# Attention and a gated feed-forward block in one kernel: stores, loads, casts and PSUM banks moved in a hand-written order

## The chip, the cores and the metric

One Trainium2 chip, one of its cores. The metric is the device time in microseconds (us) of one execution of the kernel; lower is better. The core has a matrix engine (TensorE, PE in the profile), a vector engine (VectorE, DVE), an activation engine (ScalarE, ACT), a general engine (GpSimd, POOL) and a queue engine (SyncE, SP) from which this kernel issues every DMA. Each executes its own instructions strictly in the order in which the program gives them to it; semaphores hold an instruction until its data or its buffer is there.

## The reference

```python
B, H, S, D = 8, 12, 448, 64
scores = (q @ k.T) / sqrt(D) - log(S)          # per batch b and head
attn = sigmoid(scores)
x = (attn @ v)                                  # heads side by side: 3584 tokens x 768
h = x @ w_in                                    # 768 x 2048
g = h * clip(h + 3, 0, 6) / 6
out = g @ w_out                                 # 2048 x 768, float32
```

The weights arrive as 64-bit floating-point numbers, as pairs of 32-bit words.

## The kernel before, in words

**Three stages on PE.** *Attention* is 168 steps. A step (`scores`, lines 167 to 178) multiplies one 128-wide piece of keys of a head pair with all queries into one of two PSUM score banks (tag `sc`), and ACT takes its sigmoid (line 177) into a buffer `a`. Two steps later (`LAG`) `av` (lines 180 to 205) multiplies that with the values into the PSUM bank of the head pair. After the last piece ACT copies one half of the bank (line 202), DVE adds the other half (line 203), and when three head pairs of a half batch are done, the result goes to DRAM (line 205) for batches 2 to 7.

*The first product*, x @ w_in (FFN1 below), and *the second*, g @ w_out (FFN2), are done on blocks with Strassen's scheme in Winograd's form: 7 block products M1 to M7 instead of 8, each on sums or differences of blocks. Both factors of a product are split in a rounded high part (ACT, `CAST`, line 69) and a low part (DVE, line 70), and three matmuls are done for each pair: high x high, high x low, low x high.

FFN1 is 112 slots, written out by `slots()` (lines 81 to 87): for column groups q = 0 to 15 the seven products, in an order that mixes group q+1 with the end of group q: M1(q+1), M4(q), M2(q+1), M3(q), M6(q+1), M5(q+1), M7(q+1). A slot (`product`, line 319) is 18 matmuls. M1, M6, M7 and M4 accumulate in a bank A (two buffers `sc`), M2 in a bank B, M5 and M3 in a bank D. ACT copies A after M1, M6 and M7 (lines 356 to 358; names `s`, `u`), since the next product adds to the same bank; DVE adds the copies to B or D (line 362, `cB`, `cD`), ACT takes a relu (line 353), DVE the gate (line 344), POOL two differences of the gated blocks (lines 367, 369), and SP stores them (line 349).

FFN2 is 56 units: products in the order M1, M2, M6, M7, M5, M4, M3 (`PHASES`), for each four groups p and two halves h. A unit is 36 matmuls into a bank triple `po`. Its moving part `gx` is loaded (`gr`, line 428, for M5 and M4 with two more pieces, line 433, that DVE subtracts, line 443), cast and split. After the second half DVE or ACT adds the bank to running sums (line 573 or 590) and SP stores finished outputs (line 576).

**Beside them: the weights.** `decode` (lines 46 to 64) turns the 64-bit pairs into 32-bit numbers: one ACT operation (line 50, absolute value), then six on DVE (lines 52 to 63). w_in is decoded during attention in 16 pieces (`w1_unit`, line 228; four POOL sums per two pieces, lines 75 to 78; stores, lines 242 and 243), the first half of w_out during attention (`w2_unit`, line 245), its second half in units 0 to 11 of FFN2, followed by four POOL sums (`w2_sums`, lines 528 to 531) and five stores (line 536), twice. Each piece is a generator; an `events` table calls its next stage at a given step.

**Order and buffers.** The order is by hand: every engine gets its instructions in program order. Weight loads of both kinds (`wi`, `wo`, and `ws`, `w2s` for FFN1 and FFN2) use one pool of three staging buffers (line 135); split FFN1 weights, the decoded blocks and the second pieces for M5 and M4 one ring of five (line 138). The load of slot n+5's weights is issued at slot n (line 493) and its cast and low part at slot n+2, three slots ahead of use (line 494). `at_slot` and `at_unit` are tables like `events`, for FFN1 and FFN2. A buffer that is asked for again is waited for by the first instruction that writes it.

Of the kernel before, what the change touches and what calls it, by code (L numbers as in the profile page):

```python
# [18 lines left out]
P = 128  # L19
# [47 lines left out]
def split(nc, hi, lo, a):  # L67

    nc.scalar.copy(hi, a)  # L69
    nc.vector.tensor_tensor(out=lo, in0=a, in1=hi.bitcast(F32), op=ALU.subtract)  # L70

# [19 lines left out]
def tile_kernel(ctx: ExitStack, tc: tile.TileContext, qk, vP, wi, wo, outT):  # L91
# [56 lines left out]

    ops, at, pv, xr = {}, {}, {}, {}
# [30 lines left out]
    def av(n):  # L180
        pair, c = step(n)
        a = at.pop(n)
        for p in pair:
            if p not in pv:
                pv[p] = bank(f"pv{p % 2}", 1, f"pv_{p}")
# [10 lines left out]
        if c is None or (p % 2 and c == NC - 1):  # L196
# [7 lines left out]
            if k == KC - 1 and b >= 2:  # L204
                nc.sync.dma_start(out=xd[b, u], in_=xr.pop((b, u)))
# [17 lines left out]
    def x_split(p, k):  # L223
        x = xt[k].tile([P, 2, KC, S], F32R, tag="x", name=f"x_{p}_{k}")
        split(nc, x[:, 0], x[:, 1], xr[p].pop(k))
        xts[p, k] = x

    def w1_unit(j, fh, held):
# [8 lines left out]
        if fh:  # L237
            s = ring(f"wS_{j}", [P, 4, KW], F32)
            sums(nc.gpsimd, *(a[:, k] for k in range(4)), *(s[:, k] for k in range(4)))
            yield  # L240
            q, r = divmod(j, 2)
            nc.sync.dma_start(out=dw1[q][:, :4, r], in_=a)
            nc.sync.dma_start(out=dw1[q][:, 4:, r], in_=s)

    def w2_unit(k, h, ec, held):
# [7 lines left out]
        if ec == EC - 1 and k in (A11, A12):  # L253
            nc.sync.dma_start(out=dw2[k, h], in_=held.pop((k, h)))
# [46 lines left out]
    for s in range(NS + LAG):  # L301
        if s < NS:
            scores(s)
        for f, a in events.get(s, []):
# [7 lines left out]
    later = {}  # L312

    def at_slot(n, f, *a):
        later.setdefault(n, []).append((f, a))
# [3 lines left out]
    def product(i, q, n):  # L319
# [101 lines left out]

    def g_load(n):
        if n >= len(units):
            return
        i, p, h = units[n]
        first, second = {T1: (B12, B11), T4: (B21, T2)}.get(MOVING[i], (MOVING[i], None))
        t = gset[n % 3].tile([P, FC, S], F32, tag="gr", name=f"gr_{n}")
        nc.sync.dma_start(out=t, in_=gd[p, first, h])
        others = []
        if second is not None:  # L430
            for k in range(2):
                o = ring(f"gr_{n}_{k}", [P, 2, S], F32)
                nc.sync.dma_start(out=o, in_=gd[p, second, h][:, 2 * k : 2 * k + 2])
                others.append(o)
        gr[n] = t, others

    def g_split(n):
        if n >= len(units):
            return
        t, others = gr.pop(n)  # L440
        for k, o in enumerate(others):
            part = t[:, 2 * k : 2 * k + 2]
# [234 lines left out]
```

## Time and profile before

| What | us |
|---|---|
| median of 3 runs | 1166.34 |
| lowest, highest | 1165.04, 1167.83 |
| the profiled execution's own time | 1161.64 |
| its span in the profile | 1159.8 |
| PE busy | 1101.3 (95%) |
| DVE busy | 734.7 (63%) |
| ACT busy | 557.5 (48%) |
| POOL busy | 205.8 (18%) |

How to read it: busy times count compute instructions; matmuls are pipelined, so a matmul's own duration (some 0.37 us) is longer than the time from one to the next. "A <- B: 10.2, 8, 2.4" in a view of waits says that A stood still for B for 10.2 us in total, 8 times, 2.4 at the longest. A row of the timeline has start, length, engine, line, operation, tiles (out<-in) and, in square brackets, the idle time before it and what ended it. SPq and the like are the queue's own instructions, the DMA issues among them; for them the length includes the wait. The granted clock is the share of PE's full clock.

### The profile page before, as it was taken

The page shows a single profiled execution, that of the slowest core. Times are in us where ns is not written, and L with a number is a line of the kernel's source. Part 1 is how long each engine was busy: PE and PEld are TensorE (multiplying, and loading weights), DVE is VectorE, ACT ScalarE, POOL GpSimd, SP SyncE. Part 2 cuts the span into 40 slices and gives each one's busy share as a digit, 9 for nine tenths or more (in the row PEclk, how much of TensorE's full clock was granted, in tenths as well). Part 3 has the DMA queues.
Part 4 walks back from the last instruction along what each step waited for, and adds up shares of the span by engine and source line. Part 5 has one row for each costly group of instructions (what it writes and reads, how often), then busy time and mean ns, then how long its engine had stood idle before and what let it go on. Part 6 is the DMA issues. An engine that isn't in the chain of part 4 may idle for free. (4 is left out here: it accounts for less than half of the span.)

```text
span 1159.8 us, 16568 instructions
## 1 busy us (share of the span) xinstructions
PE 1101.3 (95%) x6720; PEld 864.8 (75%) x6720; DVE 734.7 (63%) x710; ACT 557.5 (48%) x612; POOL 205.8 (18%) x90
## 2 busy tenths in 40 slices
PE   8998998999999999999999998978989999989997
PEld 3433333344898899888988997968979998979997
DVE  4579654652576788777777677848643437776531
ACT  6787776886445544645554454332232313222320
POOL 1123120000143155226221113050600000000000
PEclk9999999999999999999999999998999999999999
DMA  6866978874776777587666688956775364786641
GB/s 252 307 259 229 335 275 297 313 258 163 260 227 200 268 226 238 163 304 230 200 192 213 210 259 292 348 214 236 297 290 182 127 233 171 292 312 261 252 170 60
DMA packets 81740, 278.70 MB, mean 240 GB/s; under 512 B 7936, under 2 KB 22272, under 8 KB 81664
## 3 DMA queue, kind: packets, MB, share of 16 engines
q1 hardware_dynamic: 81664, 277.64, 68.0%
q8 instruction: 53, 0.87, 0.3%
q14 instruction: 23, 0.19, 0.0%
HBM read 190.71 MB, written 86.90 MB: 239 GB/s over the span
## 5 line engine op out<-in xcount | busy, mean ns | idle before, releaser
L634 PE MATMUL po<-gx,w 128*128 128x448 f32 x2016 | 419.9, 370 | 21.2 <-DVE w L70 10.7
L634 PEld LDWEIGHTS po<-gx,w 128*128 128x128 f32 x2016 | 380.3, 189 | 60.8 <-DVE w L70 12.8
L333 PE MATMUL A<-x,w 128*128 128x448 f32 x1152 | 241.2, 367 | 0.7 <-ACT s L358 0.7
L333 PEld LDWEIGHTS A<-x,w 128*128 128x128 f32 x1152 | 216.0, 188 | 21.3 <-ACT s L358 1.1
L69 ACT CAST gx<-gr 128x1792 fp32r<-128x1792 f32 x56 | 94.8, 1694 | 258.8 <-PE po L634 98.8
L70 DVE TENSOR_TENSOR gx<-gr,gx 128x1792 fp32r<-128x1792 f32 x56 | 122.2, 2183 | 121.7 <-ACT gx L69 121.6
L177 ACT ACTIVATE a<-sc,bias_s 128x896 f32<-128x896 f32 x168 | 168.1, 1010 | 46.6 <-PE sc L175 44.2
L70 DVE TENSOR_TENSOR w<-ws,w 128x768 fp32r<-128x768 f32 x112 | 148.4, 1334 | 53.4 <-ACT w L69 53.4
L175 PE MATMUL sc<-qk 64*64 64x448 f32 x1344 | 163.7, 549 | 18.0 <-ACT a L177 12.4
L192 PE MATMUL pv<-a,v 64*64 64x448 f32 x1344 | 163.0, 542 | 2.6 <-DVE xr L203 2.3
L333 PE MATMUL D<-x,w 128*128 128x448 f32 x576 | 126.4, 374 | 10.2 <-DVE cD L362 10.2
L333 PEld LDWEIGHTS D<-x,w 128*128 128x128 f32 x576 | 110.1, 192 | 22.7 <-issue 13.0
L175 PEld LDWEIGHTS sc<-qk 64*64 64x64 f32 x1344 | 51.9, 135 | 99.4 <-issue 56.3
L192 PEld LDWEIGHTS pv<-a,v 64*64 64x64 f32 x1344 | 53.5, 134 | 79.9 <-issue 72.8
L69 ACT CAST w<-ws 128x768 fp32r<-128x768 f32 x112 | 92.1, 828 | 19.9 <-DMA ws<-dw 19.8
L367 POOL TENSOR_TENSOR gT<-g,g 128x896 f32<-128x896 f32 x16 | 43.8, 2735 | 287.2 <-DVE g L344 181.8
L353 ACT ACTIVATE g<-cD,bias 128x896 f32<-128x896 f32 x32 | 33.5, 1045 | 77.6 <-issue 39.1
L203 DVE TENSOR_TENSOR xr<-pv,y 128x448 f32<-128x448 f32 x48 | 29.8, 621 | 53.8 <-ACT y L202 53.6
L333 PE MATMUL B<-x,w 128*128 128x448 f32 x288 | 61.4, 366 | 0.0
L333 PEld LDWEIGHTS B<-x,w 128*128 128x128 f32 x288 | 54.1, 188 | 4.7
L344 DVE SCALAR_TENSOR_TENSOR g<-g,cD 128x896 f32<-128x896 f32 x32 | 46.4, 1451 | 16.2 <-ACT g L353 16.2
L358 ACT COPY u<-A 128x896 f32<-128x896 f32 x32 | 28.9, 904 | 46.9 <-PE A L333 46.9
(57 smaller groups left out, 741.6 us busy)
## 6 DMA issues: line engine op xcount, KB each, us to landing
gr<-gd SPq DMA_DIRECT2D x56, 896.0 KB, 6.0
ws<-dw SPq DMA_DIRECT2D x112, 384.0 KB, 4.0
gd<-g SPq DMA_DIRECT2D x64, 448.0 KB, 4.7
qk<-qk SPq DMA_DIRECT2D x48, 448.0 KB, 6.7
gd<-gT SPq DMA_DIRECT2D x32, 448.0 KB, 4.7
gr<-gd SPq DMA_DIRECT2D x32, 448.0 KB, 6.6
wi<-wi SPq DMA_DIRECT2D x16, 768.0 KB, 8.0
wo<-wo SPq DMA_DIRECT2D x24, 512.0 KB, 6.2
```

The source lines that it names most:

```text
L69: nc.scalar.copy(hi, a)
L70: nc.vector.tensor_tensor(out=lo, in0=a, in1=hi.bitcast(F32), op=ALU.subtract)
L175: nc.tensor.matmul(out, k[halves[r], at_k], q[halves[r]], start=True, stop=True)
L177: nc.scalar.activation(a, sc[:, :, :S], AF.Sigmoid, bias=bias_s, scale=scale)
L192: nc.tensor.matmul(pv[p][halves[j], r, :S], v, a[halves[r], int(r != j) if c is None else j], start=first, stop=last)
L203: nc.vector.tensor_tensor(out=xr[b, u][:, k], in0=pv[p][:, 1, :S], in1=y, op=ALU.add)
L333: nc.tensor.matmul(t[:, j, :S], w[:, wk, j, kc], x[:, xk, kc], start=i in (M1, M2, M5) and m == 0, stop=m == 3 * KC - 1, skip_group_check= ...
L344: nc.vector.scalar_tensor_tensor(out=r, in0=r, scalar=6.0, in1=h, op0=ALU.min, op1=ALU.mult)
L353: nc.scalar.activation(r, h, AF.Relu, bias=bias_3, scale=1.0)
L358: nc.scalar.copy(acc[key, q], acc["A", q][:, :, :S])
L367: nc.gpsimd.tensor_tensor(out=t3, in0=quad[q, B22], in1=quad[q, B12], op=ALU.subtract)
L634: nc.tensor.matmul(po[p][:, ec, :S], w[:, wk, c], x[:, xk, c], start=h == 0 and c == 0 and xk == 0 and wk == 0, stop=h == 1 and c == FC - ...
```

## The change

The same block products with the same operands; what moves is when instructions are given out.

1. **Splits in two.** `split` becomes a generator: cast, then at a later point the low part. In attention and FFN1 the low part comes one step or slot after its cast. In FFN1 the cast stays three slots ahead, the low part is two ahead. In FFN2 the cast of unit n+2 is issued before the other work of unit n, the low part behind it; weight splits issue three casts, then three low parts.
2. **Stores later.** Weight stores in attention are issued three steps after the sums (w_out two after the decode), activation stores three steps after the last addition, finished outputs one unit after the addition (`at_unit(n + 1, put, ...)`).
3. **Loads earlier.** Pieces of w_in 8 steps before their decode instead of 4 (which itself is two steps later), w_out 6 instead of 3; `gr` at unit n for n+4 instead of n+3; FFN2's first weights at slots 90 and 91 instead of 100 and 101, split at 94 to 97 instead of 102 and 104.
4. **The second half of w_out.** A piece's ACT operation is issued a unit before its DVE operations. Three of the four sums are on DVE, one on POOL. The second group starts at unit 9 instead of 6, and one of its blocks goes from the sum into the split without a store and a load (`w2_direct`).
5. **Banks B and D** (and the two banks of the head pairs in attention) share one tag with two buffers instead of a tag with one buffer each.
6. **The end.** The last output is stored in three pieces.

```diff
 def split(nc, hi, lo, a):
     nc.scalar.copy(hi, a)
+    yield
     nc.vector.tensor_tensor(out=lo, in0=a, in1=hi.bitcast(F32), op=ALU.subtract)
+    yield
...
-                pv[p] = bank(f"pv{p % 2}", 1, f"pv_{p}")
+                pv[p] = bank("pv", 2, f"pv_{p}")
...
             if k == KC - 1 and b >= 2:
-                nc.sync.dma_start(out=xd[b, u], in_=xr.pop((b, u)))
+                on(n + LAG + 3, x_store, b, u)
...
             sums(nc.gpsimd, *(a[:, k] for k in range(4)), *(s[:, k] for k in range(4)))
-            yield
             q, r = divmod(j, 2)
+            for _ in range(4):
+                yield
             nc.sync.dma_start(out=dw1[q][:, :4, r], in_=a)
             nc.sync.dma_start(out=dw1[q][:, 4:, r], in_=s)
...
         if ec == EC - 1 and k in (A11, A12):
+            yield
+            yield
             nc.sync.dma_start(out=dw2[k, h], in_=held.pop((k, h)))
...
     for u in range(4 * NQ):
-        todo.append((1 + 6 * u, 4, w1_unit(*divmod(u, 2), held)))
+        todo.append((3 + 6 * u, 8, w1_unit(*divmod(u, 2), held)))
     for u in range(4 * EC):
         kh, ec = divmod(u, EC)
-        todo.append((101 + 4 * u, 3, w2_unit(*divmod(kh, 2), ec, held)))
+        todo.append((103 + 4 * u, 6, w2_unit(*divmod(kh, 2), ec, held)))
...
     for s, lead, gen in todo:
-        on(max(0, s - lead), next, gen, None)
-        for k in range(6):
-            on(s + k, next, gen, None)
+        over(on, [max(0, s - lead), *range(s, s + 10)], gen)
...
     for i, k in enumerate((B11, B22, B21, T3, T1, T2, T4)):
-        on(end0 + 6 + 2 * i, x_split, 0, k)
+        over(on, (end0 + 6 + 2 * i, end0 + 7 + 2 * i), x_split(0, k))
     for n in range(LA):
-        on(NS - 8 + 2 * n, w1_load, n)
-        on(NS - 4 + 2 * n, w1_split, n)
+        on(NS - 10 + n, w1_load, n)
+        over(on, (NS - 3 + n, NS - 2 + n), w1_split(n))
...
         if i == M2:
-            acc["B", q] = bank("pv0", 1, f"B_{q}")
+            acc["B", q] = bank("pv", 2, f"B_{q}")
         if i == M5:
-            acc["D", q] = bank("pv1", 1, f"D_{q}")
+            acc["D", q] = bank("pv", 2, f"D_{q}")
...
         for i in range(7):
-            at_slot(last[i, p - 1] + 1, x_split, p, MOVING[i])
+            over(at_slot, (last[i, p - 1] + 1, last[i, p - 1] + 2), x_split(p, MOVING[i]))
     end = len(seq)
+    for n in range(LA, end):
+        over(at_slot, (n - LA, n - LA + 1), w1_split(n))
     for h in range(2):
-        at_slot(end - 12 + h, w2_load, M1, h)
-        at_slot(end - 10 + 2 * h, w2_split, M1, h)
+        at_slot(end - 22 + h, w2_load, M1, h)
+        over(at_slot, (end - 18 + 2 * h, end - 17 + 2 * h), w2_split(M1, h))
...
+    at_slot(last[M6, p_last] + 1, g_load, 0)
+    over(at_slot, (last[M6, p_last] + 3, last[M6, p_last] + 4), g_split(0))
+    at_slot(last[M2, p_last] + 1, g_load, 1)
+    over(at_slot, (end, end), g_split(1))
...
-        w1_split(n + LA)
         product(i, q, n)
...
     g_load(2)
+    g_load(3)
...
     def w2_sums(h):
         a = [held.pop((k, h)) for k in range(4)]
         s1 = ring(f"w2S1_{h}", [P, EC, FC * P], F32)
-        t = nc.gpsimd
-        t.tensor_tensor(out=s1, in0=a[A21], in1=a[A22], op=ALU.add)
-        t.tensor_tensor(out=a[A21], in0=a[A11], in1=a[A21], op=ALU.subtract)
-        t.tensor_tensor(out=a[A11], in0=s1, in1=a[A11], op=ALU.subtract)
-        t.tensor_tensor(out=a[A12], in0=a[A12], in1=a[A11], op=ALU.subtract)
+        nc.vector.tensor_tensor(out=s1, in0=a[A21], in1=a[A22], op=ALU.add)
+        nc.vector.tensor_tensor(out=a[A21], in0=a[A11], in1=a[A21], op=ALU.subtract)
+        nc.vector.tensor_tensor(out=a[A11], in0=s1, in1=a[A11], op=ALU.subtract)
+        nc.gpsimd.tensor_tensor(out=a[A12], in0=a[A12], in1=a[A11], op=ALU.subtract)
...
-    for h in range(2):
+    for h, n in ((0, 0), (1, 9)):
         for e in range(2 * EC):
             k, ec = divmod(e, EC)
-            gen = w2_unit(A21 + k, h, ec, held)
-            at_unit(max(0, 6 * h + e - 1), next, gen, None)
-            at_unit(6 * h + e, drain, gen)
-        at_unit(6 * h + 4, w2_reload, h)
-        at_unit(6 * h + 6, w2_sums, h)
-        at_unit(6 * h + 7, w2_store, h)
+            u = n + e
+            over(at_unit, [max(0, u - 1), u, u + 1, u + 1, u + 1, u + 1], w2_unit(A21 + k, h, ec, held))
+        at_unit(n + 4, w2_reload, h)
+        at_unit(n + 2 * EC + (h == 0), w2_sums, h)
+        at_unit(n + 2 * EC + 2, w2_store, h, *((S1, A22, S3, S2) if h == 0 else (S1, A22, S3)))
+        at_unit(n + 2 * EC + 3, w2_store, h, S4)
     for k, i in enumerate(PHASES[1:]):
         n = 8 * (k + 1)
-        at_unit(n - 2, w2_load, i, 0)
-        at_unit(n - 1, w2_load, i, 1)
-        at_unit(n - 1, w2_split, i, 0)
-        at_unit(n, w2_split, i, 1)
+        for h in range(2):
+            if (i, h) == (M6, 1):
+                at_unit(n, w2_direct, i, h)
+            else:
+                at_unit(n - 2 + h, w2_load, i, h)
+            over(at_unit, (n - 1 + h, n - 1 + h), w2_split(i, h))
...
-        g_split(n + 2)
-        g_load(n + 3)
+        g_load(n + 4)
+        g_load2(n + 3)
+        low = None
+        if n + 2 < len(units):
+            g_sum(n + 2)
+            low = g_split(n + 2)
+            next(low)
         for f, a in plan.pop(n, []):
             f(*a)
+        if low is not None:
+            next(low)
```

`over(when, steps, gen)` enters one call of the generator's next stage at each of the given steps. `g_sum` holds the subtractions that `g_split` began with; `g_load2` loads their second operands.

More of the change, by code (lines that the diff above doesn't have):

```diff
@@ L147, in raw, with on, at_slot, at_unit @@
         return xs.tile([P, KC, S], F32, tag="xraw", name=name, bufs=5)
+    events, later, plan = {}, {}, {}
+    def on(s, f, *a):
+        events.setdefault(s, []).append((f, a))
+    def at_slot(n, f, *a):
+        later.setdefault(n, []).append((f, a))
+    def at_unit(n, f, *a):
+        plan.setdefault(n, []).append((f, a))
+    def over(when, steps, gen):
+        for n in steps:
+            when(n, next, gen, None)
     ops, at, pv, xr = {}, {}, {}, {}
@@ L303, in tile_kernel @@
             scores(s)
-        for f, a in events.get(s, []):
+        for f, a in events.pop(s, []):
             f(*a)
@@ L310, in tile_kernel @@
             load(p)
-    later = {}
-    def at_slot(n, f, *a):
-        later.setdefault(n, []).append((f, a))
+    for s in sorted(events):
+        for f, a in events.pop(s):
+            at_slot(s - NS - LAG + 1, f, *a)
     acc, quad = {}, {}
@@ L422, in g_load @@
     def g_load(n):
[L423 to L430, printed above, removed]
-            for k in range(2):
-                o = ring(f"gr_{n}_{k}", [P, 2, S], F32)
-                nc.sync.dma_start(out=o, in_=gd[p, second, h][:, 2 * k : 2 * k + 2])
-                others.append(o)
@@ L435, in g_load @@
-        gr[n] = t, others
-    def g_split(n):
[L438 to L442, printed above, removed]
-            nc.vector.tensor_tensor(out=part, in0=part, in1=o, op=ALU.subtract)
-        x = gset[n % 3].tile([P, 2, FC, S], F32R, tag="gx", name=f"gx_{n}")
-        split(nc, x[:, 0], x[:, 1], t)
-        gs[n] = x
+        if n < len(units):
+            i, p, h = units[n]
+            first, _ = PARTS.get(MOVING[i], (MOVING[i], None))
+            gr[n] = gset[n % 3].tile([P, FC, S], F32, tag="gr", name=f"gr_{n}")
+            nc.sync.dma_start(out=gr[n], in_=gd[p, first, h])
@@ new lines, in g_load2, with g_sum @@
+    def g_load2(n):
+        if n < len(units) and MOVING[units[n][0]] in PARTS:
+            i, p, h = units[n]
+            gs[n] = [ring(f"gr_{n}_{k}", [P, 2, S], F32) for k in range(2)]
+            for k in range(2):
+                nc.sync.dma_start(out=gs[n][k], in_=gd[p, PARTS[MOVING[i]][1], h][:, 2 * k : 2 * k + 2])
+    def g_sum(n):
+        for k, o in enumerate(gs.pop(n, ())):
+            part = gr[n][:, 2 * k : 2 * k + 2]
+            nc.vector.tensor_tensor(out=part, in0=part, in1=o, op=ALU.subtract)
@@ L460, in w2_split @@
             flat = w.rearrange("p t c e -> p t (c e)")
-            split(nc, flat[:, 0], flat[:, 1], st[:, ec])
             w2[i, h, ec] = w
+            gens.append(split(nc, flat[:, 0], flat[:, 1], st[:, ec]))
+        for _ in range(2):
+            for g in gens:
+                next(g)
+            yield
     last = {}
@@ L483, in xt_close @@
         g_open()
-    for n in range(LA):
-        pass
     for n in range(LA, LA + 2):
@@ L513, in tile_kernel @@
     )
-    def drain_later():
-        for n in sorted(later):
-            for f, a in later.pop(n):
-                f(*a)
-            if later:
-                return
-    gA = {}
-    def w2_sums(h):
-        a = [held.pop((k, h)) for k in range(4)]
-        s1 = ring(f"w2S1_{h}", [P, EC, FC * P], F32)
-        t = nc.gpsimd
-        t.tensor_tensor(out=s1, in0=a[A21], in1=a[A22], op=ALU.add)
-        t.tensor_tensor(out=a[A21], in0=a[A11], in1=a[A21], op=ALU.subtract)
-        t.tensor_tensor(out=a[A11], in0=s1, in1=a[A11], op=ALU.subtract)
-        t.tensor_tensor(out=a[A12], in0=a[A12], in1=a[A11], op=ALU.subtract)
-        gA[h] = {A22: a[A22], S1: s1, S2: a[A11], S3: a[A21], S4: a[A12]}
-    def w2_store(h):
-        for k in (S2, S3, S1, A22, S4):
-            nc.sync.dma_start(out=dw2[k, h], in_=gA[h].pop(k))
+    made = {}
     def w2_reload(h):
@@ L619, in tile_kernel @@
+            stt(o, t, so[other])
+            if i == M5:
+                stt(so[p], t, so[p])
+            at_unit(n + 1, put, p, eh, k, o)
+    for n, (i, p, h) in enumerate(units):
+        if n == 0:
+            for _ in range(2):
+                for f, a in later.pop(min(later)):
+                    f(*a)
+        elif n == 1:
             while later:
-                drain_later()
+                for f, a in later.pop(min(later)):
+                    f(*a)
             tmp_ctx.close()
```

105 lines of the change are left out of this document (40 added, 65 removed).

## The prediction

> **What bounds the kernel now.** I read the page, then the busy time by stretches, then who TensorE (PE) waited for, then the queues of ScalarE (ACT), VectorE (DVE) and SyncE (SP) behind those waits.
>
> ```profile
> span 1159.8 us, 16568 instructions
> 0.00:284.30 284.30, 263.75 (x2689) 104.28 (x2689) 164.43 (x229) 216.27 (x255) 39.26 (x38) 0.99 0.74 270
> 217.00:283.00 66.00, 66.00 (x704) 26.48 (x696) 30.50 (x54) 53.62 (x65) 0.00 (x0) 1.00 0.68 247
> 284.30:712.60 428.30, 417.36 (x2020) 380.18 (x2016) 311.00 (x249) 217.94 (x250) 127.45 (x42) 0.99 0.71 229
> 303.00:370.00 67.00, 67.00 (x331) 61.79 (x331) 44.31 (x38) 34.19 (x40) 24.17 (x8) 1.00 0.70 215
> 622.00:700.00 78.00, 78.00 (x378) 70.82 (x378) 53.62 (x49) 39.83 (x49) 19.54 (x8) 1.00 0.75 236
> 715.40:1154.00 438.60, 419.95 (x2016) 380.32 (x2016) 254.75 (x229) 123.24 (x107) 39.09 (x10) 0.98 0.62 232
> 860.00:960.00 100.00, 100.00 (x489) 91.41 (x488) 42.85 (x28) 25.47 (x20) 0.00 (x0) 1.00 0.51 182
> ```
>
> Each row is a stretch, its length, then busy time and instruction count of PE, its weight loads, DVE, ACT and GpSimd (POOL), the granted clock and DMA. PE bounds every stage; the others have room. Stretches without a stall give its pace: 66/704 = 0.0938 us a matmul in attention, 67/331 = 0.202 to 78/378 = 0.206 in the first product (FFN1), 100/489 = 0.2045 in the second (FFN2). For all matmuls that is 2688 x 0.0938 = 252, 2016 x 0.202 to 0.206 = 408 to 416, and 412 us. Against the stages, 32, 12 to 20 and 26 us are lost. A slot of FFN1 (18 matmuls) is 3.7 us, a unit of FFN2 (36) 7.4, a step of attention (16) 1.5.
>
> ```profile
> PE sc L175 <- ACT a L177: 12.4, 11, 3.8
> PE po L634 <- DVE w L70: 10.7, 5, 5.8
> PE D L333 <- DVE cD L362: 10.2, 8, 2.4
> PE po L634 <- ACT w L69: 7.9, 3, 4.6
> PE sc L175 <- DMA qk<-qk: 5.5, 3, 4.4
> PE po L634 <- DVE g L344: 2.6, 1, 2.6
> 402.37 0.44 PE L333 MATMUL D<-x,w 128*128 128x448 f32 x1 [1.84 <-DVE cD L362]
> 403.70:407.10 3.40, 3.40 (x11) 3.00 (x10) 2.52 (x3) 3.12 (x4) 0.00 (x0) 0.50 1.03 413
> 779.10:789.40 10.30, 4.21 (x10) 3.29 (x11) 10.10 (x14) 4.73 (x6) 0.00 (x0) 0.50 0.83 292
> ```
>
> PE's waits are few and long. Some cost twice: after the idle 1.84 us at 402 the granted clock is 0.50 for 3.4 us, worth 1.7 us more. Whether a gap does that depends on more than its length (no such row follows the 2.6 us at line 344), so I charge 1.7 us behind each new single gap above 3 us and none behind shorter ones. The Trainium skill, "TensorE: Matmul & The Clock Gate", section "Why this matters for your kernels", asks for no PE gap above about 3 us between bursts. By it the gap of 1.84 us would have left the clock whole; the row at 403 says otherwise. By the page alone, the 1.7 us behind that gap would not be there to win.
>
> **Attention: stores later, loads earlier.**
>
> ```profile
> ACT wA L50 <- DMA wi<-wi: 14.6, 8, 4.2
> SPq L242 <- DVE wA L63: 68.0, 8, 11.9
> SPq L243 <- POOL wS L78: 36.2, 8, 7.7
> 138.25 0.48 SPq L231 DMA_DIRECT2D wi<-wi  x1
> 142.56 0.90 ACT L50 ACTIVATE wA<-wi 128x768 f32<-128x768 f32 x1 [2.28 <-DMA wi<-wi]
> L177 ACT ACTIVATE a<-sc,bias_s 128x896 f32<-128x896 f32 x168 | 168.1, 1010 | 46.6 <-PE sc L175 44.2
> L69 ACT CAST x<-xr 128x1344 fp32r<-128x1344 f32 x16 | 20.9, 1308 | 0.0
> ```
>
> ACT executes in order. An absolute value (line 50) whose load has not landed holds the next sigmoid, and PE needs that sigmoid. The loads are late because SP, also in order, sits at a store until DVE (68.0 us) or POOL (36.2 us) has made its data: the load issued at 138.25 lands after ACT has stood for 2.28 us. The change issues weight stores three steps after their sums and activation stores three steps later (4.5 us each), and loads weights 8 steps ahead instead of 4 (output weights 6 instead of 3). That is 4.5 to 6 us more, above the longest wait of 4.2, and none of these stores sits in front any more: I count ACT's load waits as gone. Staging does not prevent it: a load for unit u goes out at step 6u-5, its buffer was last read at step 6u-12. What stays: at steps 50 to 63 seven casts (1.31) join 14 sigmoids (1.01). With two or three absolute values (0.9) and four copies (0.5) ACT has 14.1 + 9.2 + 4.3 = 27.6 us for 21 us of PE steps; two score banks absorb about 1.5, so 5 us stay lost whatever loads do. Splitting cast and low part over two steps takes DVE's waits away there, not ACT's work. Of 12.4 + 1.1 (query loads without the first, 4.4) + 2 clock windows of 1.7 = 17 us named, 5 stay; of the unnamed rest, short gaps behind each stall, I count 4 as gone. **-16 us** (-8 if ACT's queue and not the loads is the limit; -20 if nearly all goes).
>
> **FFN1.**
>
> ```profile
> DVE w L70 <- ACT w L69: 53.7, 32, 7.0
> SPq L271 <- DVE w L70: 274.4, 101, 6.6
> L69 ACT CAST w<-ws x112: 814/829/842, 278.2 to 699.6; 128x768 fp32r<-128x768 f32 x112
> L70 DVE TENSOR_TENSOR w<-ws,w x112: 944/952/2893, 279.0 to 703.6; 128x768 fp32r<-128x768 f32 x112
> DMA to landing us min/median/max: 3.1/4.0/10.4
> L358 ACT COPY u<-A 128x896 f32<-128x896 f32 x32 | 28.9, 904 | 46.9 <-PE A L333 46.9
> ```
>
> (The three rows with slashes give min, median and max: ns, the landing us.) Before, the low part (line 70) stands on DVE right behind its cast: DVE idles 53.7 us for it, and the sum cD (line 362) that frees bank D comes late for M5, 10.2 us of PE. Now the low part runs a slot after its cast, so these idles go and cD comes about 2 us into the slot after M3, of 3.7 allowed. Should the shared pair hand M5 the bank that B left two slots earlier, the wait goes even if cD stays late. **-10.2, and two clock windows, -3.4.** Low parts still lie two slots (7.4 us) ahead of PE.
>
> The cost is in staging: three buffers. A weight load must wait for the low part three loads earlier, now a slot later; 4.0 + 0.83 + 0.95 = 5.8 us per round in a buffer that has 3 x 3.7 stays harmless. But the first FFN2 weights now take two of the three buffers at slots 90 and 91 and return them with their low parts at 95 and 97 (before: taken at 100 and 101, returned at 102 and 104). In between one buffer is left, and each load waits for the one before it, 5.8 us for a slot of 3.7. The load for slot 96 leaves about 2 us into slot 93; two rounds later that for slot 98 leaves, lands (4.0) and is cast (0.83): 2 + 11.6 + 4.8 = 18.4. The copy of M7's result stands behind that cast on ACT (0.9): 19.3. M4 of slot 97, which writes over that bank, starts at 4 x 3.7 = 14.9: **+4.4, with its clock window +6** (+1.7 with landings of 3.1 instead of 4.0; 0 if ACT's casts get ahead). Net **-8** (-14 to -2).
>
> **The seam.** PE waits 2.6 us for a gate (line 344) that stands on DVE behind the low part of unit 1; that part moves behind the gates: **-2.6.** Unit 1 is still ready: cast 1.7 and low 2.0 fit in unit 0's 7.4.
>
> **FFN2.**
>
> ```profile
> ACT w L50 <- POOL w2r L531: 13.1, 1, 13.1
> L214 DVE TENSOR_TENSOR xT<-xr,xr x1: 1550/1550/1550, 79.7 to 79.7; 128x1344 f32<-128x1344 f32 x1
> 782.13 0.42 DVE L52 TENSOR_SCALAR w<-w 128x512 f32<-128x512 f32 x1
> 784.96 0.69 DVE L63 TENSOR_TENSOR w<-w,wo 128x512 f32<-128x512 f32 x1
> 817.86 3.53 POOL L528 TENSOR_TENSOR w2S<-w,w 128x1536 f32<-128x1536 f32 x1 [41.84 <-DVE w L63]
> 819.50 3.77 DVE L70 TENSOR_TENSOR gx<-gr,gx 128x1792 fp32r<-128x1792 f32 x1 [0.31 <-ACT gx L69]
> L70 DVE TENSOR_TENSOR w<-w2s,w 128x512 fp32r<-128x512 f32 x42 | 28.4, 730 | 0.4 <-ACT w L69 0.4
> L443 DVE TENSOR_TENSOR gr<-gr,gr 128x896 f32<-128x896 f32 x32 | 33.7, 1086 | 5.4 <-DMA gr<-gd 5.2
> L573 DVE SCALAR_TENSOR_TENSOR s<-po,s 128x1344 f32<-128x1344 f32 x12 | 18.6, 1554 | 23.6 <-PE po L634 23.6
> L69 ACT CAST gx<-gr 128x1792 fp32r<-128x1792 f32 x56 | 94.8, 1694 | 258.8 <-PE po L634 98.8
> ```
>
> PE's 10.7 + 7.9 = 18.6 us sit at three places. (a) Units 7 and 8: ACT stands 13.1 us at an absolute value that needs a ring buffer, held until POOL's four sums are made and stored; PE loses the longest waits, 4.6 and 5.8, and the 0.50 clock of the row at 779 costs about 2 more. Three of the four sums go to DVE (1550 x 1536/1344 = 1.77 each), the second half starts at unit 9 instead of 6, behind the stores of unit 8. DVE ends unit 7's sums about 2 us into it, its weight low parts by 6, PE needs them at 7.4: -12.4. (b) Units 15 to 17, 3.3 plus a window 1.7: unit 15 now holds on DVE the last decode (3.5, rows 782 to 785), three sums (5.3) and then the weight low part (0.7) of unit 16. From 0.4 us before the unit that ends 9.1 into it, 1.7 late; the fourth sum on POOL (3.5) then holds up the second low part, as the row at 819 shows (3.77 beside POOL, 2.02 without): 1.7 more. +3.4 for 5.0. (c) Phase M5 to M4, units 33 to 41, 5.0: the loads stand behind output stores on SP. These stores now wait one unit and loads go a unit earlier, but DVE's round of two units stays full: two s/o updates (3.1), four subtractions (4.3), two low parts (4.0), and two casts that it waits for (3.4), 14.8 of 14.8. The weight low parts, now ahead of the moving one, save unit 40; for unit 41 the first is ready 3.5 us late, since updates, subtraction, cast of 1.7 and weight cast still precede it. With its window 5.2 for 5.0. Sum of (a) to (c): **-13.6** (-22 if neither (b) nor (c) stalls; -6 if (a) keeps half).
>
> **The end.** The last result goes out in thirds, but the last third is issued after the same last update: -0.5.
>
> **The sum.** -16 - 8 - 2.6 - 13.6 - 0.5 = -40.7. The profiled execution took 1161.64 (1.84 beside its span) and would become 1120.9; the median of the runs, 1166.34, lies 4.7 above it, so I state 1166.3 - 40.7, about 1125.
>
> **The rivals.**
> - *No new stall* (18%): landings near 3.1 and DVE ahead take away the staging stall (6) and (b), (c) (8.6): 1111. For it: DVE is idle in 27% of FFN1 (311 of 428).
> - *ACT remains the limit* (17%): casts and sigmoids in one queue keep PE waiting, half of the attention and FFN2 gains goes: 1125 + 8 + 7 + 6 = 1146. For it: ACT is busy 216 of 284 us. Against: its waits are for loads.
> - *D is not freed earlier* (8%): the shared pair alternates B, D as two single buffers do and DVE stays late: + 13.6, 1139.
> - *Slower* (5%): with low parts a slot later, the staging round itself becomes FFN1's pace: (landing + 0.83 + 0.95)/3 per slot. It breaks even at a slot of 3.7 + 40.7/112 = 4.1, a landing of 10.5 us; at 11.5 every slot takes 4.4, +79 on -41, 1204. The longest landing is 10.4, the median 4.0: unlikely.
>
> **How the numbers follow.** The forecast has 52%. Differences under 0.2% (2.3 us) are about what a measurement of this kernel cannot tell from no change. All cases but the slower and a sliver (2%) of the second rival end well below 1164: faster 0.93, same 0.02, slower 0.05. The range runs from 1103 (no new stall, 1111, with the larger attention gain, 4, and FFN1 at 0.202 a matmul throughout, 4) to 1150 (ACT the limit, 1146, with FFN1 at 0.206 throughout).
>
> **What would show it.** Right: ACT's waits for wi and wo near zero; SP no longer waiting for POOL's sums in attention; D without PE wait; one or two FFN1 slots of 6 to 8 us near slot 97; units 7 and 8 at 7.4; a long unit 16 or 41. Wrong: PE still behind ACT outside the seven casts, or weight loads that land over 8 us throughout.

## The result and the profile after

| | before | after |
|---|---|---|
| median (lowest to highest), us | 1167.09 (1165.04 to 1168.53) | 1111.65 (1108.19 to 1116.47) |
| profiled execution, us | 1161.64 | 1116.47 |
| end of attention / length of FFN1 with the seam / of FFN2 / the rest, us | 284.3 / 431.1 / 438.2 / 6.2 | 263.7 / 423.5 / 422.5 / 5.0 |

The ratio of the times is 0.9529, 95% interval [0.9489, 0.9569]: faster by about 55 us. The profiled executions are only 45 us apart: before's lies under the runs of that comparison, after's is the longest of its four. Stage by stage they differ by 20.6 + 7.6 + 15.7 + 1.2.

Who PE waits for in the kernel after (total us, times, longest), and its stages (stretch, length, busy time and count of PE, its weight loads, DVE, ACT, POOL, granted clock, DMA share, GB/s):

```profile
PE A L345 <- ACT u L370: 4.8, 1, 4.8
PE sc L192 <- DMA qk<-qk: 4.4, 1, 4.4
PE po L630 <- ACT w L69: 3.4, 2, 3.2
PE po L630 <- DVE w L71: 2.5, 2, 1.3
PE pv L209 <- DVE xr L220: 2.0, 2, 1.5
PE sc L192 <- ACT a L194: 0.6, 2, 0.4
```

```profile
0.00:263.70 263.70, 256.36 (x2688) 105.46 (x2689) 162.26 (x229) 216.23 (x255) 37.88 (x38) 1.00 0.80 293
80.00:98.00 18.00, 15.97 (x164) 5.53 (x160) 17.83 (x17) 17.50 (x21) 7.01 (x4) 1.00 0.58 204
263.70:687.20 423.50, 418.57 (x2021) 380.72 (x2018) 316.46 (x249) 219.79 (x249) 125.74 (x42) 0.99 0.72 232
587.44:609.76 22.32, 22.32 (x109) 20.28 (x108) 16.69 (x13) 11.41 (x14) 5.45 (x2) 1.00 0.61 217
643.40:665.29 21.89, 21.89 (x110) 20.31 (x109) 14.33 (x12) 10.30 (x12) 5.49 (x2) 1.00 0.81 250
687.20:1109.70 422.50, 416.51 (x2017) 379.20 (x2015) 263.63 (x230) 124.65 (x108) 13.56 (x4) 1.00 0.67 239
```

The 12.4 us for sigmoids are down to 0.6, the 10.2 for cD and the 2.6 for a gate are gone, the 18.6 in FFN2 are 5.9. One row is new: 4.8 us in FFN1 for a copy u. The rows at 587 and 643 are six slots each, PE without an idle: 22.32/6 = 3.72 and 21.89/6 = 3.65 us a slot at the same granted clock of 1.00; more on that below.

**The new stall, at slot 97**, in the timeline of the kernel after (SP's rows are DMA issues):

```profile
622.46 0.83 ACT L69 CAST w<-ws 128x768 fp32r<-128x768 f32 x1 [5.03 <-DMA ws<-dw]
624.31 0.32 SPq L294 DMA_DIRECT2D ws<-dw  x1
628.17 0.83 ACT L69 CAST w<-ws 128x768 fp32r<-128x768 f32 x1 [3.32 <-DMA ws<-dw]
628.91 0.90 ACT L370 COPY u<-A 128x896 f32<-128x896 f32 x1
629.86 3.36 PE L345 MATMUL A<-x,w 128*128 128x448 f32 x8 [4.81 <-ACT u L370]
```

The load of slot 98's weights goes out at 624.31, behind the low part of the load before it; its cast stands on ACT until it has landed, the copy of M7's result stands behind that cast, and M4 behind the copy. From 628.50 to 635.30 the granted clock is 0.50. Slots 96 and 97 take 8.63 + 6.25 us, 7.4 more than two of 3.72.

**FFN2's two stalls**, in unit 16 and ahead of unit 41: the timeline, and the three low parts in the view of instructions (min/median/max in ns, first and last start):

```profile
806.62 5.19 DVE L71 TENSOR_TENSOR w<-w2s,w 128x512 fp32r<-128x512 f32 x3
806.83 3.82 POOL L534 TENSOR_TENSOR w2r<-w2r,w2r 128x1536 f32<-128x1536 f32 x1 [60.93 <-DVE w2r L533]
807.35 2.73 PE L630 MATMUL po<-gx,w 128*128 128x448 f32 x12 [1.32 <-DVE w L71]
811.25 2.11 PE L630 MATMUL po<-gx,w 128*128 128x448 f32 x9 [1.17 <-DVE w L71]
995.26 1.68 ACT L69 CAST gx<-gr 128x1792 fp32r<-128x1792 f32 x1 [7.92 <-DVE gr L448]
996.85 1.65 ACT L69 CAST w<-w2s 128x512 fp32r<-128x512 f32 x3
997.51 2.98 PE L630 MATMUL po<-gx,w 128*128 128x448 f32 x7 [3.19 <-ACT w L69]
```

```profile
L71 DVE TENSOR_TENSOR w<-w2s,w x3: 679/683/3982, 806.6 to 811.1; 128x512 fp32r<-128x512 f32 x3
```

The first low part of unit 16's weights starts at 806.62, behind DVE's sums, and PE waits 1.32 us for it; the second takes 3.98 us beside POOL's sum instead of 0.68, and PE waits 1.17 more. At 995 the weight casts stand behind the moving part's cast, which waited 7.92 us for DVE's subtraction.

### The profile page after: what moved, and what is told of

Read it like the earlier page. It is cut to its first block, busy times and chain, and to the rows that moved or that the text cites. A ratio compares the mean times of both kernels' runs of the same rounds, so it can differ in the third digit from the quotient of the medians.

```text
span 1114.7 us, 16569 instructions
## 1 busy us (share of the span) xinstructions
PE 1091.8 (98%) x6720; PEld 865.4 (78%) x6720; DVE 744.0 (67%) x710; ACT 560.7 (50%) x612; POOL 177.2 (16%) x84
## 4 chain that ended last, share of the span: by engine, by line
PE 84%; DVE 9%; ACT 3%; DMA 3%; issue 2%; SPq 0%; DVEq 0%; ACTq 0%
PE po L630 28%; PE A L345 21%; PE D L345 10%; PE sc L192 10%; PE pv L209 10%; PE B L345 5%; DVE gr L448 2%; ACT gx L69 2%; DVE gx L71 1%; DVE w L71 1%; DMA ws<-dw 1%; DVE x L71 1%; DMA w2s<-dw 1%; DVE o L567 1%; ACT w L69 0%
## 5 line engine op out<-in xcount | busy, mean ns | idle before, releaser
L630 PE MATMUL po<-gx,w 128*128 128x448 f32 x2016 | 416.9, 369 | 6.0 <-ACT w L69 3.4
L345 PE MATMUL A<-x,w 128*128 128x448 f32 x1152 | 245.7, 371 | 4.9 <-ACT u L370 4.8
L192 PE MATMUL sc<-qk 64*64 64x448 f32 x1344 | 191.5, 542 | 5.0 <-DMA qk<-qk 4.4
L209 PE MATMUL pv<-a,v 64*64 64x448 f32 x1344 | 190.4, 537 | 2.3 <-DVE xr L220 2.0
L71 DVE TENSOR_TENSOR w<-ws,w 128x768 fp32r<-128x768 f32 x112 | 154.1, 1385 | 32.2 <-ACT w L69 31.9
L71 DVE TENSOR_TENSOR gx<-gr,gx 128x1792 fp32r<-128x1792 f32 x56 | 113.2, 2022 | 70.5 <-ACT gx L69 70.5
L192 PEld LDWEIGHTS sc<-qk 64*64 64x64 f32 x1344 | 63.9, 134 | 80.5 <-issue 62.9
L209 PEld LDWEIGHTS pv<-a,v 64*64 64x64 f32 x1344 | 64.3, 133 | 77.0 <-issue 69.8
L345 PE MATMUL D<-x,w 128*128 128x448 f32 x576 | 123.9, 368 | 0.0
L374 DVE TENSOR_TENSOR cD<-D,u 128x896 f32<-128x896 f32 x32 | 34.8, 1088 | 24.9 <-ACT u L370 15.7
```

What stands on the lines that cost most here:

```text
L192: nc.tensor.matmul(out, k[halves[r], at_k], q[halves[r]], start=True, stop=True)
L209: nc.tensor.matmul(pv[p][halves[j], r, :S], v, a[halves[r], int(r != j) if c is None else j], start=first, stop=last)
L345: nc.tensor.matmul(t[:, j, :S], w[:, wk, j, kc], x[:, xk, kc], start=i in (M1, M2, M5) and m == 0, stop=m == 3 * KC - 1, skip_group_check= ...
L374: nc.vector.tensor_tensor(out=c, in0=acc[name, q][:, :, :S], in1=acc[key, q], op=ALU.add)
L630: nc.tensor.matmul(po[p][:, ec, :S], w[:, wk, c], x[:, xk, c], start=h == 0 and c == 0 and xk == 0 and wk == 0, stop=h == 1 and c == FC - ...
```

## The experiments

Times are medians of 4 to 6 executions, ratios are against the kernel before on the same chip. Experiments 1, 2, 3 and 10 ran on one chip, 4 and 7 to 9 on a second, 5, 6 and 11 on a third, 12 on a fourth; the kernel before took 1168.2, 1165.6, 1164.4 and 1166.9 us on them, so a few us between experiments of different chips mean little. Edits are to the kernel after (12's to the kernel of 11).

**1. The same kernel again.**

> The changed kernel once more, as a control beside the next three. Its first profiled execution took 1116.5 us while three others took 1108.2 to 1112.7, so a second trace should tell what differs from run to run. My theory: the three new stalls (about 4.8 us at slot 97 of the first product, 2.8 us in unit 16 and 3.3 us at unit 41 of the second) come from the order of the program and stand there again within 1 us each; what varies is the pace of the matmuls, 93 slots of 3.72 us there and 13 of 3.65 (worth up to 6.5 us). Rival: the stalls themselves come and go with the landing times of the loads, and the run-to-run spread is theirs.

1111.76 us (1109.41 to 1113.43), 0.9524 [0.9489, 0.956]. The same three stalls (5.0, 3.4, 2.5), so they belong to the program; attention 264.7, FFN2 422.9. FFN1 is 416.9 instead of 423.5: 93 slots ran at 3.65 and 14 at 3.72, in the profile above 13 and 94 (the others are the long ones). That is (94 - 14) x 0.07 = 5.6 of the 6.6 us between the two FFN1s; whether the runs without a profile spread by it is not shown.

**2. FFN2's first weights staged late, at slots 100 and 101.**

```diff
-        at_slot(end - 22 + h, w2_load, M1, h)
-        over(at_slot, (end - 18 + 2 * h, end - 17 + 2 * h), w2_split(M1, h))
+        at_slot(end - 12 + h, w2_load, M1, h)
+        over(at_slot, (end - 10 + 2 * h, end - 9 + 2 * h), w2_split(M1, h))
```

> One part undone: the second product's first weights go into the staging buffers at slots 100 and 101 again and are split at 102 to 105, instead of 90, 91 and 94 to 97. My theory: the wait of 4.8 us for the copy before slot 97 and the 0.50 clock of 6.8 us behind it come from two of three staging buffers held for five slots; held for three they are gone, with at most 1 us left near slot 105: 7 to 8 us less than the changed kernel. Rival: the copy is late because the casts of the second product's weights stand in front of it on the activation engine; then a stall of 3 us or more moves to about slot 105 and the time stays within 3 us of the changed kernel.

1104.83 us (1103.6 to 1111.19), 0.9475 [0.944, 0.951]. The row for the copies u is gone; what is left of FFN1's waits:

```profile
PE A L345 <- ACT s L370: 0.7, 1, 0.7
```

FFN1 is 409.6, the half clock at slot 97 is gone, and only 0.8 us are lost at slot 104. So two of three staging buffers, lent out ten slots early, cost 7 us, about 1 of them by the slots behind the stall, which ran at 3.72 in experiment 1 and at 3.65 here.

**3. B and D, and the head pairs' banks, back in one buffer each.**

```diff
-                pv[p] = bank("pv", 2, f"pv_{p}")
+                pv[p] = bank(f"pv{p % 2}", 1, f"pv_{p}")
...
-            acc["B", q] = bank("pv", 2, f"B_{q}")
+            acc["B", q] = bank("pv0", 1, f"B_{q}")
...
-            acc["D", q] = bank("pv", 2, f"D_{q}")
+            acc["D", q] = bank("pv1", 1, f"D_{q}")
```

> One part undone: banks B and D (and the two banks of a head pair) have one buffer each again; all else as changed. My theory: the wait of the matrix engine for the sum cD, 10.2 us before, went because the low parts no longer make the vector engine wait, so it comes back by at most 2 us in all, and the time is within 0.3% of the changed kernel. Rival: the shared pair is what took it away, M5 gets the bank that B left earlier; then the wait for cD is 8 to 10 us again and the time 10 us or more above the changed kernel.

1112.14 us (1109.53 to 1117.21), 0.953 [0.949, 0.9569]; FFN1 418.2, no wait for cD. With casts and low parts apart, sharing the buffers moves nothing that can be measured.

**4. Casts and low parts of FFN1's weights together again, ahead of the slot's other work.**

```diff
-        over(at_slot, (n - LA, n - LA + 1), w1_split(n))
+        over(at_slot, (n - LA, n - LA), w1_split(n))
```

> One part undone in the first product: the low part of a weight stands directly behind its cast again, both three slots ahead of use; the shared banks stay. My theory: the vector engine idles for the casts again (53.7 us in the kernel before, 32 in the changed one), but M5 takes the bank that B left, so the late sum cD costs the matrix engine little: less than 3 us against the changed kernel, after the pace of the slots is taken out; the staging stall at slot 97 gets shorter, since each round in the one free buffer no longer waits for the next slot's place in the queue. Rival: with the low parts late again the copies and sums are late and 8 to 10 us of waits return, at M5 or, since its bank is free, at M7.

1138.86 us (1136.41 to 1140.54), 0.978 [0.9753, 0.9807]: 27 us of the gain gone (by the ratios 0.978 and 0.9524, 30), FFN1 441.1. My theory (under 3 us) was wrong; the wait is not for D either, but for the copies u. Waits and timeline of this kernel:

```profile
PE A L345 <- ACT u L370: 22.7, 11, 4.1
```

```profile
407.65 0.96 DVE L71 TENSOR_TENSOR w<-ws,w 128x768 fp32r<-128x768 f32 x1 [1.90 <-ACT w L69]
409.53 1.08 DVE L374 TENSOR_TENSOR cD<-D,u 128x896 f32<-128x896 f32 x1
410.69 1.04 ACT L365 ACTIVATE g<-cD,bias 128x896 f32<-128x896 f32 x1 [3.08 <-issue]
412.37 0.89 ACT L370 COPY u<-A 128x896 f32<-128x896 f32 x1
413.31 4.88 PE L345 MATMUL A<-x,w 128*128 128x448 f32 x15 [2.21 <-ACT u L370]
```

Two in-order queues in a circle: DVE stands at the low part for ACT's cast, the sum cD stands behind it, ACT's relu, for which ACT has stood 3.08 us, starts as cD ends (409.53 + 1.08 = 410.61; the relu at 410.69), and the copy that PE wants stands behind that relu and one more cast.

**5. Together, but behind the slot's gates and relus, as before the change; 6. the same with one buffer each for B and D.**

```diff
-    for n in range(LA, end):
-        over(at_slot, (n - LA, n - LA + 1), w1_split(n))
...
         w1_load(n + LA + 2)
+        if n + LA < end:
+            for _ in w1_split(n + LA):
+                pass
```

> The casts and low parts of the FFN1 weights stay together in one slot, but behind the gates and relus of that slot instead of ahead of them, as in the kernel before; the shared pair of buffers stays. The run with them together and ahead showed 22.7 us of PE waits for the copies u on ACT and an FFN1 of 441.1 us against 416.9. Theory: there DVE stood at each low part for its cast with the sums cD and cB behind it, and ACT stood at the relus for these sums (67.5 and 58.7 us of ACT's waits, against 25.5 and 39.7 with the parts apart) with the copies and casts behind them: a circle of the two queues. Behind the gates the circle is half open: FFN1 of 424 to 433 us, and PE waits of 5 to 15 us, for D or for u, beside the one at slot 97. Rival, the place in the slot is all that cost: FFN1 within 3 us of 417 and no PE wait but that at slot 97.

> As fused_behind, and B and D go back to one buffer each, so that bank D is bound to M5 as before the change. If sharing removes PE's wait for D when low parts stand behind their casts: PE waits for cD of 8 to 12 us, and FFN1 5 to 14 us longer than with the shared pair. If sharing is worth nothing there too: the same FFN1 within 2 us, and the same kind of wait in both.

5: 1115.33 us (1113.88 to 1116.84), 0.9578 [0.9561, 0.9595], FFN1 418.7. 6: 1117.81 us (1116.92 to 1120.88), 0.9603 [0.9584, 0.9621], FFN1 427.0. The wait that 5 has not and 6 has:

```profile
PE D L345 <- DVE cD L374: 3.6, 2, 1.8
```

So of the 27 us of experiment 4 most, 23.5, came from the place in the slot, not from the pairing: the rival was right for 5, but for 2.5 us of PE's waits that are not at slot 97. In 6 the wait for D comes back, at 3.6 us with two stretches at half clock (1.7 each). The two medians are only 2.5 us apart and the intervals of their ratios overlap; the 8.3 us between the FFN1s are more because the profile of 6 is of its longest run, with some 25 more slots at 3.72 (1.8 us). By the waits, then, sharing the buffers does help where low parts follow their casts at once, and is idle where they don't; the times alone do not show it. My 8 to 12 us was too much: the splits of x stayed apart in both kernels, and what they do of before's 10.2 was not tried.

**7. Loads with their old lead; 8. stores at their old place; 9. both.**

```diff
-        todo.append((3 + 6 * u, 8, w1_unit(*divmod(u, 2), held)))
+        todo.append((3 + 6 * u, 4, w1_unit(*divmod(u, 2), held)))
...
-        todo.append((103 + 4 * u, 6, w2_unit(*divmod(kh, 2), ec, held)))
+        todo.append((103 + 4 * u, 3, w2_unit(*divmod(kh, 2), ec, held)))
```

```diff
-            for _ in range(4):
-                yield
+            yield
             nc.sync.dma_start(out=dw1[q][:, :4, r], in_=a)
...
-            yield
-            yield
             nc.sync.dma_start(out=dw2[k, h], in_=held.pop((k, h)))
...
-                on(n + LAG + 3, x_store, b, u)
+                x_store(b, u)
```

> One part undone in attention: the pieces of w_in are loaded 4 steps before their decode again instead of 8, those of w_out 3 instead of 6; the stores stay late. My theory: both parts count. A piece of w_in lands 7.8 us after its issue (median), four steps are 6 us, so the activation engine waits up to 2 us for most of the 28 pieces, two score banks absorb about 1.2 us of each, and attention, which ends at 264 to 265 us in the changed kernel and at 284 before, ends 6 to 10 us later. Rival A: the stores alone blocked the queue; then attention stays within 2 us. Rival B: the lead is everything; then attention ends at 280 or later.

> The other part undone in attention: weight stores and activation stores stand directly behind their data again; the loads stay 8 and 6 steps ahead. My theory: the queue stands at a store for up to 11.9 us as before, a lead of 12 us for a piece that lands in 7.8 us leaves 4 us for that, so the longest waits return, mostly in the first 110 us: attention ends 3 to 7 us later than in the changed kernel. Rival A: within 2 us, since the longer lead absorbs any store. Rival B: 12 us or more, since the blocked queue was the cause.

> Both parts of attention undone together: stores at once, loads 4 and 3 steps ahead; the split of cast and low part stays two steps, and all later stages stay as changed. My theory: attention is back near 284 us, within 4 us, since the order of cast and low part adds little there; FFN1 and FFN2 stay as in the changed kernel. Rival: cast and low part on two steps are what won most of the 20 us; then attention ends at 275 or earlier.

7: 1117.86 us (1117.8 to 1118.16), 0.9602 [0.9575, 0.963], attention ends at 270.6. 8: 1120.72 us (1120.02 to 1121.63), 0.9627 [0.9603, 0.965], 272.6. 9: 1134.97 us (1134.4 to 1136.31), 0.975 [0.9726, 0.9774], 285.2. The waits of 7, then of 8:

```profile
PE sc L192 <- ACT a L194: 5.0, 6, 2.7
ACT wA L50 <- DMA wi<-wi: 5.7, 2, 3.5
```

```profile
PE sc L192 <- DMA qk<-qk: 10.5, 4, 4.5
SPq L225 <- DVE xr L220: 69.0, 10, 13.1
```

Against an end of 264.7 (experiment 1) the leads undone alone cost 6 us, the stores 8, both together 20.5: the whole gain of this stage, and more than the sum. With short leads ACT meets loads that have not landed; with early stores it is the query loads behind them on SP that come late. Either cure covers part of the other's ill.

**10. FFN2's weight parts ahead of the moving part.**

```diff
+    ahead = {}
+
+    def at_front(n, f, *a):
+        ahead.setdefault(n, []).append((f, a))
...
-                at_unit(n, w2_direct, i, h)
+                at_front(n, w2_direct, i, h)
...
-            over(at_unit, (n - 1 + h, n - 1 + h), w2_split(i, h))
+            over(at_front, (n - 1 + h, n - 1 + h), w2_split(i, h))
...
         g_load2(n + 3)
+        for f, a in ahead.pop(n, []):
+            f(*a)
         low = None
```

> One thing moved: in the second product the weight splits of the next phase are issued ahead of the other work of their unit (ahead of the subtractions and the cast of the moving part, and in unit 15 ahead of the last decode and the three sums). My theory: units 16 and 41 are late because the vector engine reaches the low parts of the weights last; with the weights first, both are on time, 1.5 + 1.3 and 3.3 us of waits and the 0.50 clock of 3.4 us at unit 41 go: 7 to 8 us less than the changed kernel. Rival: the vector engine has too much to do there in any order; then the wait moves to the moving parts of units 17 and 42 and less than 3 us are won.

1106.59 us (1104.11 to 1114.62), 0.949 [0.9454, 0.9525]. FFN2 is 418.0, 4.5 to 4.9 less than in the two profiles of the kernel after, between the 7 to 8 of the theory and the rival's 3: unit 16 is no longer late, the 3.19 us ahead of unit 41 are gone and it takes 8.09 instead of 8.86, but a wait has moved into unit 17, which takes 10.99 us:

```profile
810.27 5.91 PE L637 MATMUL po<-gx,w 128*128 128x448 f32 x20 [1.79 <-DVE w L71]
```

**11. Edits 2 and 10, the fourth sum of w_out issued two units later; 12. that sum on DVE.**

```diff
-        nc.gpsimd.tensor_tensor(out=a[A12], in0=a[A12], in1=a[A11], op=ALU.subtract)
+        fourth[h] = a[A12], a[A11]
...
+    def w2_fourth(h):
+        d, b = fourth.pop(h)
+        nc.gpsimd.tensor_tensor(out=d, in0=d, in1=b, op=ALU.subtract)
...
+        at_unit(n + 2 * EC + (1 if h == 0 else 2), w2_fourth, h)
```

```diff
-        nc.gpsimd.tensor_tensor(out=d, in0=d, in1=b, op=ALU.subtract)
+        (nc.vector if h else nc.gpsimd).tensor_tensor(out=d, in0=d, in1=b, op=ALU.subtract)
```

> The late staging of the first output weights (worth 7 us alone), the weight parts of FFN2 ahead of the moving one (worth 4.7 us of FFN2 alone), and besides the fourth sum of w_out on POOL two units later for the second half, one by itself behind the weight low parts of unit 16. Theory: with the weight parts ahead, unit 17 was 10.99 us long since its three weight low parts took 3.73 us beside POOL's sum; without POOL beside them they take about 2.2, and unit 17 falls to 7.4 to 8.6. Time 1096 to 1100. Rival, DVE's queue of unit 15 (decode, three sums) alone makes unit 17 late: it stays at 10 to 11 us, and the time is about 1100 to 1102.

> As best2, but the fourth sum of the second half of w_out runs on DVE, behind the low parts of unit 16. In best2 POOL, idle and bound to nothing but its data, began that sum at 797.22, as soon as the third sum ended, although it was issued two units later; so the three weight low parts still took 3.73 us beside it (1.294 each; 0.63 to 0.68 elsewhere) and unit 17 waited 1.8 us. On DVE the sum has its place in the queue. Theory, POOL's sum beside them is what makes these low parts slow: they take about 2.0 us together, PE's wait for DVE w of 1.8 us goes, unit 17 falls from 9.49 to 7.4 to 7.8, and the time by about 2, to 1096 to 1098. Rival, it is their operand (the buffer w2r instead of w2s): 3.7 us again, unit 17 stays at 9.5 and the time at 1099.

11: 1099.16 us (1098.05 to 1099.91), 0.9437 [0.9421, 0.9453]. Unit 17 is 9.49, outside what I expected. The edit did not do what I meant: POOL had nothing else to do and began the sum when its data was there, wherever it was issued. The low parts of 11, then the moving part's low part ahead of them, POOL's sum and PE's wait:

```profile
L71 DVE TENSOR_TENSOR w<-w2r,w x3: 678/679/2524, 800.4 to 803.5; 128x512 fp32r<-128x512 f32 x3
```

```profile
797.00 2.02 DVE L71 TENSOR_TENSOR gx<-gr,gx 128x1792 fp32r<-128x1792 f32 x1
797.22 5.16 POOL L541 TENSOR_TENSOR w2r<-w2r,w2r 128x1536 f32<-128x1536 f32 x1 [60.44 <-DVE w2r L533]
802.98 3.35 PE L644 MATMUL po<-gx,w 128*128 128x448 f32 x15 [1.83 <-DVE w L71]
```

One low part takes 2524 ns, the other two 678: the first stands until POOL's sum has ended (802.38). The sum stands too: the moving part's low part began 0.22 us ahead of it and took its usual 2.02. Without the 1.80 until that one's end at 799.02 the sum has 3.36 us, as in the kernel after, where a low part that ended at 807.30 was ahead of it: 3.82 - 0.47 = 3.35. 12: 1096.32 us (1095.58 to 1103.63), 0.9419 [0.9386, 0.9453], the lowest median here, though its interval overlaps that of 11. Its low parts:

```profile
L71 DVE TENSOR_TENSOR w<-w2r,w x3: 681/681/683, 799.4 to 800.6; 128x512 fp32r<-128x512 f32 x3
```

The same operand, no sum on POOL beside it: 0.68 each, PE's wait for them 0.6, unit 17 7.59. The Trainium skill, "SBUF — State Buffer", section "Who interferes with whom", says that a DVE instruction with two SBUF inputs contends with a GpSimd instruction that reads SBUF, and that the later one blocks until the other has ended instead of sharing. The trace agrees: 2524 ns for one, 681 to 683 once the sum is gone.

## Why the prediction was right, and where not

The predicted 1125 lies 13 us above the median, which the range holds. From one profiled execution to the other the forecast of -40.7 met -45.2 (1161.64 to 1116.47). The remaining 9 of the 13 are the anchor: I added the 4.7 by which before's median lay above its profile, and after's median lies 4.8 below its own. That before's profiled execution lies below its runs and after's is its longest is chance, and no part of the forecast. The pace of the slots makes most of the difference between after's two profiled executions (experiment 1); what spreads the other runs, before's above all, no profile shows.

- **Attention, -16 predicted, -20.6 measured.** Right: ACT's waits for weights are gone, and experiments 7 to 9 show that leads and stores make all of it. The failed term is the 5 us that ACT's queue was to lose at the seven casts. The overload exists (the row at 80: ACT 17.50 of 18.00 busy), but PE's idle of 18.00 - 15.97 = 2.0 us there is mostly not ACT's (another 0.20 for a sigmoid stands at 91.48):

```profile
88.04 0.98 PE L192 MATMUL sc<-qk 64*64 64x448 f32 x8 [0.37 <-ACT a L194]
95.42 0.98 PE L209 MATMUL pv<-a,v 64*64 64x448 f32 x8 [1.46 <-DVE xr L220]
```

Steps 50 to 63 take 24.2 us (scores at 79.55 to 103.74) where 26 were forecast, 3.2 over their pace; 1.5 of these are the wait for DVE's addition, which the kernel before had too (1.51 us). That leaves 1.7 for ACT instead of 5. The 27.6 us of ACT's work were too many because they added up lengths of records, and ACT's records overlap: a sigmoid at 83.14, an absolute value at 84.04, a sigmoid at 84.87, a cast at 85.76 and the next sigmoid at 86.96 start 0.90, 0.83, 0.89 and 1.20 us apart, each about 0.1 less than its length. With these and 0.43 for a copy the same work is 14 x 0.90 + 7 x 1.20 + 2.5 x 0.83 + 4 x 0.43 = 24.8 us, an estimate from these rows. Also wrong: that SP would stop waiting for the sums. Its queue after has 32.9 for POOL (36.2 before); only the waits for DVE are much shorter (68.0 before at the weight stores):

```profile
SPq L264 <- POOL wS L80: 32.9, 8, 6.7
SPq L225 <- DVE xr L220: 29.3, 7, 9.3
SPq L263 <- DVE wA L63: 26.2, 6, 6.1
```

The stores still hold SP, for less time; the leads of 8 steps cover part of what is left, which is why 7 and 8 do not add up.

- **D's wait, -10.2 and two clock windows: right, by a mechanism told half right.** DVE's waits in FFN1, before, after, and in experiment 4:

```profile
DVE w L70 <- ACT w L69: 49.0, 30, 7.0
DVE cB L362 <- PE B L333: 2.1, 3, 0.7
DVE cD L362 <- PE D L333: 0.7, 1, 0.7
```

```profile
DVE w L71 <- ACT w L69: 25.5, 19, 4.8
DVE cB L374 <- PE B L345: 22.0, 13, 3.1
DVE cD L374 <- PE D L345: 9.2, 11, 4.3
```

```profile
DVE w L71 <- ACT w L69: 125.2, 64, 4.8
```

Low parts still wait 25.5 us for casts, against my "these idles go". Experiment 5 shows that these idles are not what PE's wait hangs on: DVE stands 56.5 us for casts there, more than before, and PE never waits for D. What counts is that the sums now stand ready and wait for PE (2.1 and 0.7 became 22.0 and 9.2). The alternative I left open, that the shared pair removes the wait, holds only in the arrangement of experiments 5 and 6, not in this kernel (3).

- **The staging stall, +4.4 and its window, +6 together: right in place, chain and size.** 4.8 idle, 7.4 with the half clock, at slot 97; experiment 2 takes it away for 7.
- **FFN1 as a whole, -10.6 with the seam, -7.6 in the profile.** Counted from 3.65 us a slot, before's 17 slots over 3.76 hold 19.5 us, where 10.2 + 3.4 + 2.6 were to go; all of it went. After's four hold 8.1, where 6 were to come. And the pace adds (94 - 41) x 0.07 = 3.7, since 94 slots ran at 3.72 after and 41 before: -19.5 + 8.1 + 3.7 = -7.7. With the pace of experiment 1 the whole is -14.2. The prediction had both paces as an uncertainty of a stretch's matmuls and no term for it.
- **FFN2, -13.6 predicted, -15.7 measured.** (a) Units 7 and 8 take 7.39 each, as forecast. (b) Unit 16 waits 1.32 + 1.17 for its low parts where I had 1.7 + 1.7, the first behind DVE's sums, the second behind POOL's, as said; for unit 17, 12 shows that it is POOL's sum. (c) Unit 41 waits 3.19 and then runs at half clock, for the 3.5 and 1.7 predicted, with the casts in the order that was said. The 2.1 are mostly before's stalls, costed too low: over 7.39 a unit, units 7 and 8, 15 and 16, and 33 to 41 lost 12.7 + 5.4 + 6.3 us, where 12.4 + 5.0 + 5.0 were charged. Of the new ones, unit 16 lost 3.0 for 3.4 and units 39 to 41 lost 5.7 for 5.2. (The three terms of the forecast add up to -13.8, not -13.6.)
- **The rival "no new stall"** gave 1111 and the median is 1111.65. It is wrong all the same: all three stalls are in both profiles of this kernel. The time alone would have confirmed the wrong case. "ACT remains the limit" (its sum of 1146 has a 6 for which no row was given) and "slower" did not occur; weight loads land in 3.9 us at the median.

## What to carry to other kernels

In two in-order queues that feed each other, ask what stands behind each waiting instruction: the same two instructions, ahead of the slot's other work instead of behind it, cost 23.5 us (experiments 4 and 5). Before resources are claimed earlier, count how many are left for the stream that uses them all the time; two of three staging buffers, away from slot 90 to slots 95 and 97, cost 7 us. An instruction is not delayed by being issued later on an idle engine; to keep it away from another, give it a real predecessor or another engine.

## What the runs showed of the hardware that I had not expected

- FFN1's matmuls have two paces at a granted clock of 1.00, 3.72 and 3.65 us a slot (0.207 and 0.203 a matmul), and one program runs 13 or 93 of its slots in the faster one. In the profile after, the change comes at the stall of slot 97, in experiment 1 at the same place and the other way; experiments 2, 11 and 12, without that stall, run at 3.65 throughout. No experiment set the pace; its cause stays open.
- Whether a gap halves the clock is not told by its length: the gap of 1.79 us ahead of unit 17 in experiment 10 is followed by 0.50 for 3.4 us, the gap of 1.83 at the same place in 11 by none. I had charged a window only above 3 us. What tells it in these traces is where the gap lies. In every profile with more than one stretch at 0.50 these start whole multiples of 3.413 us from one another. Cut at these multiples, the 14 profiles have 35 pieces at full clock that a stretch at 0.50 follows, and PE is idle in 53% or more of each; in the 4442 that none follows it is idle in 52% at most, but for one with 58% in experiment 9 (the first 4.5 us and the end left out). The gap in 10 falls into one piece (1.61 of 3.41 us busy), the one in 11 is split over two (2.45 and 2.54):

```profile
808.17:811.58 3.41, 1.61 (x8) 1.22 (x7) 3.41 (x4) 1.67 (x1) 1.50 (x1) 1.00 0.98 382
811.60:815.00 3.40, 3.40 (x11) 3.02 (x10) 3.40 (x2) 0.00 (x0) 0.00 (x0) 0.50 0.37 66
```

```profile
798.70:802.11 3.41, 2.45 (x12) 1.90 (x11) 3.41 (x3) 3.02 (x3) 3.41 (x1) 1.00 0.62 189
802.11:805.52 3.41, 2.54 (x12) 2.35 (x13) 3.41 (x4) 0.40 (x1) 0.27 (x1) 1.00 0.73 284
803.00:815.00 12.00, 12.00 (x59) 10.98 (x60) 8.58 (x6) 1.70 (x1) 0.00 (x0) 1.00 0.78 262
```
